# Moving the first weight columns to float32 loads with casts on chip, turning a batch's tails on TensorE, holding back small loads, and issuing the output weights a step earlier, in a fused attention and feed-forward kernel

## The chip, the cores and the metric

The kernel runs on one core of one Trainium2 chip. The metric is the device time of one execution in microseconds (us). Several executions of each kernel were taken, and each experiment ran beside the kernel before on the same chip. Times inside an execution are counted from the start of its span in the profile. Engines: PE is TensorE, DVE is VectorE, ACT is ScalarE, POOL is GpSimd, SP is SyncE (which only issues transfers here); PEld stands for TensorE's weight loads. L412 is line 412 of that kernel's source; the same line has other numbers in other kernels. PSUM is the memory into which PE writes its results.

## The reference, cut to what matters

Eight batches of causal attention over 8 heads of 64, with 576 queries and 16 extra "beacon" keys and values in front of 576 keys, then a gated feed-forward layer on all 4608 rows:

```python
scores = q @ concat(beacon_k, k).T / sqrt(64)      # causal mask on the 576 x 576 part
x = softmax(scores) @ concat(beacon_v, v)          # all heads side by side: 4608 x 512
out = (relu(x @ w_gate) * (x @ w_val)) @ w_out     # 512 -> 1536 -> 512
```

All inputs are float32 in HBM. The kernel computes with bfloat16 (bf16) operands, so that every input has to be cast once.

## The kernel before

PE is to be busy all the time. Batch one's attention runs alone in seven "steps"; then some up-projections of the first 512 rows run alone (`ALONE`) while batch two's inputs arrive; from then on attention steps of the next batch and pieces of the feed-forward layer take turns on PE. `after(s, f)` puts work at the end of step `s`, `mid[s]`, `between[s]` and `behind[s]` put it inside a step. Each engine runs its own instructions in the order in which they are written.

The parts that the change and the argument touch (cuts marked `...`):

```python
def load_w(dst, src, n0, n1, groups=(0, 1)):        # casting load: float32 -> bf16 on its way,
    for g in groups:                                # issued by GpSimd
        nc.gpsimd.dma_start(dst[:, 2*g:2*g+2, n0:n1], src[2*g*P:2*(g+1)*P, n0:n1]...)

ALONE = ((0, 3, 3, 3), (4, 4))     # up-projections in the steps between batch one and batch two
...
first.beacon = first.load_rows(beacon_k[0])         # SyncE's queue, float32
for i in range(2): ...  first.load_quarter(n, i, g) # keys and queries, rows 0 to 511
for t in range(NKT): first.load("v", t)
...
def load_first_tails():                             # rows 496 to 575 of keys and queries
    tails["k"] = first.load_cast_rows(k[0, :, 496:])   # casting loads by GpSimd
    tails["q"] = first.load_cast_rows(q[0, :, 496:])
def turn_first_tails():
    for n, dst in (("k", first.kT4), ("q", first.qT4)):
        nc.sync.dma_start_transpose(dst[:, :, :rows], h[:rows])
    second.beacon = second.load_rows(beacon_k[1])   # batch two's small loads
    load_tails(second)
after(0, turn_first_tails)
...
after(1, lambda: load_w(wg, moe_w_gate, 0, 384))
mid[3] = lambda: load_w(wv, moe_w_val, 0, 384)
after(3, lambda: first.cast("v", 4, pool))
mid[5] = lambda: load_w(wg, moe_w_gate, 384, 768, (0,))
mid[6] = lambda: load_w(wg, moe_w_gate, 384, 768, (1,))
after(6, lambda: load_w(wv, moe_w_val, 384, 768))
for n0 in (768, 1152): ...                          # after(6): the other columns, both weights
after(6, lambda: load_second(0))                    # batch two's keys and queries: 4 casting loads
after(7, lambda: load_second(1))                    # 4 more
for t in range(NKT):
    after(7, lambda t=t: second.load("v", t, t == 0))         # held: see below
for t in range(NKT):
    after(s2 - 1 + t // 2, lambda t=t: second.cast("v", t, pool))
after(s2 - 1, lambda: load_wo(0, 6))                # output weights, two casting loads of 768 KB
after(s2, lambda: load_wo(6, 12))                   # s2: batch two's first step
```

A "held" load has a one-element `memset` by GpSimd on its target first, so that SyncE cannot issue it before GpSimd has got there.

## Time and profile before

| | before |
|---|---|
| median of the first 3 runs | 395.1 us (394.35 to 395.18) |
| span of the profiled run | 392.3 us |
| PE busy | 369.8 us |
| PE idle | 22.5 us (span less busy), 10.8 of it in gaps of over 0.3 us in the first 110 us |
| time at half clock in the first 110 us | 6.8 us |

A part of the 22.5 us may not be idle time: the trace has 4235 matmuls for 4291 weight loads, so the records of 56 matmuls are missing. From the gaps after 110 us (3.7 us here) I estimate about 3 us.

From the page of the kernel before: busy time by engine; then PE's busy tenths and the granted clock of TensorE in 40 slices of 9.8 us; then the chain that ended last, by engine.

```profile
PE 369.8 (94%) x4235; PEld 188.2 (48%) x4291; DVE 206.2 (53%) x340; ACT 190.6 (49%) x266; POOL 130.0 (33%) x224
...
PE   7949996999999999999999999999999999999994
...
PEclk9999998999999999999999999999999999999998
...
PE 84%; DMA 8%; issue 3%; POOL 2%; SPq 1%; DVE 1%; ACT 0%; POOLq 0%; DVEq 0%
```

The digits 4 and 6 in PE's row are the third and the seventh slice, near 20 to 30 and 60 to 70 us. The view of waits, for PE in the first 110 us, names them (engine, line, what was waited for: us in total, times, longest):

```profile
PE f L477 <- DMA wo<-in_moe_w_out_dram: 3.5, 1, 3.5
PE os L412 <- issue: 3.5, 1, 3.5
PE s L362 <- DMA qT<-half: 1.7, 1, 1.7
```

The second of them is odd. PE's timeline (start, duration, engine, line, operation, tiles, count, idle time before it) shows it inside the matmuls of one chunk, whose operands were all there:

```profile
24.56 0.25 PE L412 MATMUL ab<-e,v 128*32 128x80 bf16 x8
28.29 0.26 PE L412 MATMUL os<-e,ones 128*32 128x80 bf16 x4 [3.48 <-issue]
```

The last mask (`AFFINE_SELECT`) ends at 25.7 us, and from 26.4 us on GpSimd issues one casting load after the other:

```profile
25.26 0.46 POOL L378 TENSOR_SCALAR_AFFINE_SELECT e<-e 128x320 bf16<-128x320 bf16 x1 [0.60 <-ACT e L370]
...
26.40 1.42 POOL L337 DMA_DIRECT2D wv<-in_moe_w_val_dram  x2
27.82 1.43 POOL L337 DMA_DIRECT2D wg<-in_moe_w_gate_dram  x2
```

The chain of waits in order of time between 40 and 70 us (start, us, what):

```profile
42.48 0.09 POOL raw L241
...
42.97 5.62 DMA raw<-in_v_dram
...
49.11 1.23 POOL v L259 x2
...
54.21 10.57 DMA wo<-in_moe_w_out_dram
...
64.82 2.29 PE f L477 x6
```

GpSimd's `memset` lets the values of batch two go, GpSimd casts them, and only then issues the second half of the output weights, for which PE waits.

The windows view has, for each stretch, the busy time of each engine (with counts), the granted clock, the DMA share and GB/s. With the stops at 24.8 and 61.3 us the clock is halved (0.50) for 3.4 us, from 27.7 and from 65.3 us:

```profile
28.00:31.00 3.00, 2.50 (x90) 1.90 (x92) 1.94 (x4) 0.00 (x0) 3.00 (x5) 0.50 1.17 151
65.00:68.50 3.50, 3.50 (x26) 1.32 (x28) 0.00 (x0) 1.34 (x2) 2.57 (x5) 0.54 0.91 204
```

### The profile page before, as it was taken

The numbers are of one execution on the slowest core, as the hardware profiler recorded it, in microseconds if no ns is written. First come the engines' busy times: TensorE is split into PE (matmuls) and PEld (weight loads), VectorE is DVE, ScalarE is ACT, GpSimd is POOL, SyncE is SP. The second block draws the span as 40 slices with busy tenths as digits, with TensorE's granted clock in tenths as the row PEclk, the third lists the DMA queues.
The fourth block names the chain that finished last, engine by engine and source line by source line (L and its number), as shares of the span: only waits on it lengthen the run. The fifth ranks groups of instructions, "written<-read, shape, count | busy, mean of one in ns | idle before, by whom it ended". The sixth has DMA issues, their size and how long they took to land.

```text
span 392.3 us, 10180 instructions
## 1 busy us (share of the span) xinstructions
PE 369.8 (94%) x4235; PEld 188.2 (48%) x4291; DVE 206.2 (53%) x340; ACT 190.6 (49%) x266; POOL 130.0 (33%) x224
## 2 busy tenths in 40 slices
PE   7949996999999999999999999999999999999994
PEld 3534452544555454544554445454545454444443
DVE  4746661663665665465646664655465555512420
ACT  4742373434755654555555554565465543323321
POOL 1987284251752335233514351426020200000000
PEclk9999998999999999999999999999999999999998
DMA  8999999978995994489438933994300020011002
GB/s 215 177 143 179 197 209 209 196 176 167 184 159 152 209 166 127 123 177 178 101 117 173 210 90 104 191 190 99 104 28 2 2 82 27 2 54 56 0 28 85
DMA packets 148835, 49.91 MB, mean 127 GB/s; under 512 B 134320, under 2 KB 144304, under 8 KB 148784
## 3 DMA queue, kind: packets, MB, share of 16 engines
q1 hardware_dynamic: 137328, 43.27, 52.4%
q0 software_dynamic: 11456, 5.93, 11.7%
q8 instruction: 35, 0.57, 0.6%
q14 instruction: 16, 0.13, 0.1%
HBM read 38.34 MB, written 9.44 MB: 122 GB/s over the span
## 4 chain that ended last, share of the span: by engine, by line
PE 84%; DMA 8%; issue 3%; POOL 2%; SPq 1%; DVE 1%; ACT 0%; POOLq 0%; DVEq 0%
PE f L477 24%; PE f L458 22%; PE s L467 12%; PE f L467 11%; PE ab L412 6%; PE s L362 6%; DMA wo<-in_moe_w_out_dram 3%; PE os L412 3%; DMA raw<-in_v_dram 1%; DMA wide<-in_q_dram 1%; DMA qT<-half 1%; DMA half<-in_k_dram 1%; POOL v L259 1%; POOL e L378 1%; SPq L622 0%
## 5 line engine op out<-in xcount | busy, mean ns | idle before, releaser
L370 ACT ACTIVATE e<-s 128x1024 bf16<-128x1024 f32 (+2 forms) x112 | 104.8, 964 | 18.7 <-PE s L362 18.4
L461 ACT ACTIVATE g<-f 128x512 f32<-128x512 f32 x108 | 64.6, 598 | 93.4 <-PE f L458 90.5
L458 PE MATMUL f<-xT,wg 128*128 128x512 bf16 x399 | 107.3, 380 | 2.6 <-issue 1.1
L378 POOL TENSOR_SCALAR_AFFINE_SELECT e<-e 128x512 bf16<-128x512 bf16 (+2 forms) x80 | 47.0, 598 | 168.5 <-ACT e L370 163.6
L477 PE MATMUL f<-wo,hT 128*128 128x512 bf16 (+1 forms) x425 | 96.0, 375 | 5.6 <-DMA wo<-in_moe_w_out_dram 3.5
L424 DVE RECIPROCAL r<-os 128x80 f32<-128x80 f32 (+2 forms) x43 | 57.6, 1340 | 60.2 <-PE os L412 60.1
L469 DVE TENSOR_TENSOR hT<-g,s 128x512 bf16<-128x512 f32 x56 | 38.5, 687 | 55.6 <-PE s L467 54.6
L467 PEld LDWEIGHTS <-wv 128*128 128x128 bf16 x432 | 42.3, 98 | 51.5 <-issue 1.2
L477 PEld LDWEIGHTS <-hT 128*128 128x128 bf16 x444 | 42.0, 98 | 51.5 <-issue 4.3
L458 PEld LDWEIGHTS <-wg 128*128 128x128 bf16 x432 | 39.6, 98 | 46.4 <-issue 1.1
L480 ACT COPY ob<-f 128x512 f32<-128x512 f32 (+1 forms) x37 | 21.3, 575 | 76.3 <-PE f L477 76.3
L469 DVE TENSOR_TENSOR hT<-g,f 128x512 bf16<-128x512 f32 x52 | 35.8, 688 | 42.3 <-PE f L467 37.8
L467 PE MATMUL s<-xT,wv 128*128 128x512 bf16 x222 | 57.2, 379 | 0.1
L467 PE MATMUL f<-xT,wv 128*128 128x512 bf16 x207 | 53.2, 379 | 0.3
L412 PE MATMUL ab<-e,v 128*32 128x80 bf16 (+4 forms) x1320 | 39.6, 234 | 0.2 <-POOL e L378 0.2
L263 POOL CAST half<-raw 128x512 bf16<-128x512 f32 (+2 forms) x60 | 36.6, 633 | 6.3 <-DMA raw<-in_q_dram 2.2
L362 PE MATMUL s<-qT,kT 64*128 64x80 bf16 (+3 forms) x704 | 35.7, 235 | 2.5 <-DMA qT<-half 1.7
L412 PE MATMUL os<-e,ones 128*32 128x240 bf16 (+4 forms) x660 | 32.4, 233 | 3.5 <-issue 3.5
L362 PEld LDWEIGHTS <-kT 64*128 64x128 bf16 x704 | 20.5, 97 | 26.8 <-issue 23.4
L412 PEld LDWEIGHTS <-v 128*32 128x32 bf16 (+1 forms) x1408 | 27.0, 100 | 9.4 <-issue 5.2
L259 POOL CAST v<-raw 128x512 bf16<-128x512 f32 (+1 forms) x40 | 26.7, 672 | 13.1 <-DMA raw<-in_v_dram 13.0
L437 DVE TENSOR_TENSOR xT<-ab,r 128x480 bf16<-128x480 f32 (+2 forms) x45 | 24.9, 554 | 0.8
(63 smaller groups left out, 138.9 us busy)
## 6 DMA issues: line engine op xcount, KB each, us to landing
out_dram<-ob SPq DMA_DIRECT2D x35, 256.0 KB, 2.2
raw<-in_q_dram SPq DMA_DIRECT2D x25, 256.0 KB, 4.8
raw<-in_v_dram SPq DMA_DIRECT2D x24, 256.0 KB, 4.8
raw<-in_k_dram SPq DMA_DIRECT2D x19, 256.0 KB, 4.6
raw<-in_v_dram SPq DMA_DIRECT2D x8, 224.0 KB, 4.3
wg<-in_moe_w_gate_dram POOLq DMA_DIRECT2D x8, 192.0 KB, 6.2
wv<-in_moe_w_val_dram POOLq DMA_DIRECT2D x8, 192.0 KB, 6.5
wo<-in_moe_w_out_dram POOLq DMA_DIRECT2D x2, 768.0 KB, 10.0
```

Source lines behind the costliest of these rows:

```text
L259: copy(self.v[:n, t].rearrange("p (h a d) -> p h a d", a=2, d=C), raw[:n].rearrange("p (h d a) -> p h a d", a=2, d=C))
L263: copy(h[:n], raw[:n])
L362: nc.tensor.matmul(self.s[:, a, c + j * n:c + (j + 1) * n], kT[rows, 2 * g + j, k0:k0 + P], qT[rows, 2 * g + j, q0:q0 + n], start=True, st ...
L370: nc.scalar.activation(e[:, :k * 4 * n].rearrange("p (k a x) -> p a k x", k=k, a=2), self.s[:, :, :k * 2 * n].rearrange("p a (k x) -> p a ...
L378: nc.gpsimd.affine_select(out=cols[:, :, :m], in_=cols[:, :, :m], pattern=[[0, 4], [1, m]], compare_op=ALU.is_ge, fill=0.0, base=base, cha ...
L412: nc.tensor.matmul(o[:, q0 - cq0:q0 - cq0 + n], w, e[:kr, 2 * (hh % 2) + hh // 2], start=(i == 0 and part != 1), stop=(i == self.last), sk ...
L424: nc.vector.reciprocal(self.r[:, :n], self.os[:, :n])
L458: nc.tensor.matmul(g[:, :n], wg[:, ki, nf * P:(nf + 1) * P], x[:, ki], start=(ki == 0), stop=(ki == KM - 1))
L461: nc.scalar.activation(gs[:, :n], g[:, :n], AF.Relu)
L467: nc.tensor.matmul(u[:, :n], wv[:, ki, nf * P:(nf + 1) * P], x[:, ki], start=(ki == 0), stop=(ki == KM - 1))
L469: nc.vector.tensor_mul(self.h[:, nf, c0:c1], gs[:, :n], u[:, :n])
L477: nc.tensor.matmul(o[:, n], self.h[:, nf, ms * P:(ms + 1) * P], wo[:, nf, n], start=(nf == 0), stop=(nf == NF - 1))
```

## The change

Its intent: the first weights should not wait for GpSimd, which has masks and casts to do; so 256 columns of both come early on SyncE's queue as float32 and are cast on chip. The tails of batch one are turned by PE, not by the DMA transpose. Batch two's small loads should not stand in the way of the early loads. One up-projection less stands before batch two, and the output weights are issued one step earlier. The core of the diff:

```diff
-        def load_rows(self, srcs):
+        def load_rows(self, srcs, held=False):
+            if held:
+                nc.gpsimd.memset(raw[:1, :1], 0.0)
...
+    def load_w_raw(src, n):      # two float32 loads by SyncE, 256 KB each
+    def cast_w(dst, raws, n, g, cast): ...
...
-    ALONE = ((0, 3, 3, 3), (4, 4))
+    ALONE = ((0, 3, 3, 2), (4, 4))
...
-        for t in range(NKT):
+        for t in range(2):
             first.load("v", t)
+        first.tails = [first.load_rows(k[0, :, 496:]), first.load_rows(q[0, :, 496:])]
+        for t in range(2, NKT):
+            first.load("v", t)
+        raw_g = load_w_raw(moe_w_gate, 256)
+        raw_v = load_w_raw(moe_w_val, 256)
...
-            load_first_tails()
...
-        after(0, turn_first_tails)       # DMA transposes, and batch two's small loads
...
         def cast_last():
             for n in "kq":
                 first.cast_quarter(n, 1, 1, dve)
+            cast_tails(first, dve)
+        def turn_first_tails(): ...      # PE transposes into one PSUM tile
         behind[1] = cast_last
         between[2] = lambda: [turn_first(n, 1, 1, dve)() for n in "kq"]
+        behind[2] = turn_first_tails
+        after(2, lambda: [held.pop(0)() for _ in range(2)])       # moves by ACT
-        after(1, lambda: load_w(wg, moe_w_gate, 0, 384))
...
-        mid[3] = lambda: load_w(wv, moe_w_val, 0, 384)
-        after(3, lambda: first.cast("v", 4, pool))
-        mid[5] = lambda: load_w(wg, moe_w_gate, 384, 768, (0,))
-        mid[6] = lambda: load_w(wg, moe_w_gate, 384, 768, (1,))
-        after(6, lambda: load_w(wv, moe_w_val, 384, 768))
+        mid[3] = lambda: load_w(wg, moe_w_gate, 256, 768, (0,))
+        after(3, lambda: load_w(wg, moe_w_gate, 256, 768, (1,)))
+        after(4, lambda: first.cast("v", 4, dve))
+        after(4, lambda: cast_w(wg, raw_g, 256, 0, dve))
+        after(4, lambda: cast_w(wg, raw_g, 256, 1, pool))
+        after(5, lambda: cast_w(wv, raw_v, 256, 0, pool))
+        after(6, lambda: cast_w(wv, raw_v, 256, 1, pool))
+        after(6, lambda: load_w(wv, moe_w_val, 256, 768))
+        def load_small():
+            second.beacon = second.load_rows(beacon_k[1], True)    # held
+            load_tails(second)
+        after(6, load_small)
...
-        after(s2 - 1, lambda: load_wo(0, 6))
-        after(s2, lambda: load_wo(6, 12))
+        after(s2 - 2, lambda: load_wo(0, 6))
+        after(s2 - 1, lambda: load_wo(6, 12))
```

More of the change, by code (lines that the diff above doesn't have):

```diff
@@ L310, in load_rows @@
             return raw, n
-        def load_cast_rows(self, srcs):
-            n = srcs.shape[1]
-            h = half.tile([P, d_model], BF16, name="half")
-            nc.gpsimd.dma_start(h[:n].rearrange("p (h d) -> p h d", d=D),
-                                srcs.rearrange("h p d -> p h d"))
-            return h, n
         def cast_rows(self, loaded, cast):
@@ L339, in load_w, with cast_w @@
                 src[2 * g * P:2 * (g + 1) * P, n0:n1].rearrange("(p a) n -> p a n", a=2))
+    def load_w_raw(src, n):
+        raws = []
+        for g in range(2):
+            raws.append(stage.tile([P, d_model], FP32, name="raw"))
+            nc.sync.dma_start(raws[g].rearrange("p (a n) -> p a n", a=2),
+                              src[2 * g * P:2 * (g + 1) * P, :n].rearrange(
+                                  "(p a) n -> p a n", a=2))
+        return raws
+    def cast_w(dst, raws, n, g, cast):
+        cast(dst[:, 2 * g:2 * g + 2, :n], raws[g].rearrange("p (a n) -> p a n", a=2))
     def load_wo(i0, i1):
@@ L603, in turn_next @@
             first.cast_quarter("q", 1, 0, dve)
-        tails = {}
-        def load_first_tails():
-            tails["k"] = first.load_cast_rows(k[0, :, 496:])
-            tails["q"] = first.load_cast_rows(q[0, :, 496:])
         def turn_third():
-            load_first_tails()
             held.pop()()
@@ L618 @@
         behind[0] = lambda: turn_first("q", 1, 0, dve)()
-        def turn_first_tails():
-            for n, dst in (("k", first.kT4), ("q", first.qT4)):
-                h, rows = tails[n]
-                nc.sync.dma_start_transpose(dst[:, :, :rows], h[:rows])
-            second.beacon = second.load_rows(beacon_k[1])
-            load_tails(second)
-        after(0, turn_first_tails)
         after(0, lambda: first.cast("v", 0, pool))
@@ L632, in cast_last, with turn_first_tails @@
                 first.cast_quarter(n, 1, 1, dve)
+            cast_tails(first, dve)
+        def turn_first_tails():
+            ps = f_ps.tile([P, 2, NP, 80], BF16, name="f")
+            for x, (h, dst) in enumerate(zip(first.tails, (first.kT4, first.qT4))):
+                held.append(first.turn_rows(h, dst[:, :, :80], act, ps[:, x]))
         behind[1] = cast_last
         between[2] = lambda: [turn_first(n, 1, 1, dve)() for n in "kq"]
-        after(1, lambda: load_w(wg, moe_w_gate, 0, 384))
+        behind[2] = turn_first_tails
+        after(2, lambda: [held.pop(0)() for _ in range(2)])
         after(2, lambda: first.cast("v", 2, pool))
         after(2, lambda: first.cast("v", 3, pool))
-        mid[3] = lambda: load_w(wv, moe_w_val, 0, 384)
-        after(3, lambda: first.cast("v", 4, pool))
-        mid[5] = lambda: load_w(wg, moe_w_gate, 384, 768, (0,))
-        mid[6] = lambda: load_w(wg, moe_w_gate, 384, 768, (1,))
-        after(6, lambda: load_w(wv, moe_w_val, 384, 768))
+        mid[3] = lambda: load_w(wg, moe_w_gate, 256, 768, (0,))
[10 more added lines that the diff above has]
+        after(6, load_small)
         for n0 in (768, 1152):
```

## The prediction

> **What bounds the kernel.** By the page, TensorE (PE) is busy 369.8 of 392.3 us and PE work is 84% of the chain that ended last, so only PE's idle time (22.5 us) and its time at a reduced clock can be won. The PE timeline and the waits put most of it into the first 70 us:
> 1. PE waits 1.67 us, from 20.3, for the DMA transpose of the query tail (chain: 1.56 us of issuing, 5.24 us of DMA).
> 2. PE stops for 3.48 us at 24.8 amid one chunk's matmuls, put down to "issue", with all operands there. The packets of the instruction queue show a 16 KB fetch that starts only at 25.8 and lands at 26.7, between weight packets of the software queue (GpSimd's DMAs). The Trainium skill ("Runtime: NRT & Kernel Launch", Instruction fetch mechanics) says that instructions are refilled in 16 KiB blocks of 256; PE had run about 480 since the fetch before. I read this stop as a late fetch.
> 3. PE waits 3.51 us at 61.3 for the second half of the output weights, issued at 54.2 and 10.6 us on their way.
> After stops 2 and 3 the granted clock is about 0.50 in 28 to 31 us and 0.57 in 65 to 69 us (windows): an estimated 1.2 and 1.7 us lost. Together 11.6 us: the ceiling.
>
> **What the change does.** The tails come as float32 rows, are cast by VectorE (about 0.4 us each), turned by PE (16 short matmuls) and moved by ScalarE (two copies, 0.45 us each, estimated from 0.59 us for 512 columns): both transposes and two casting DMAs (0.86 and 0.73 us of issuing on GpSimd) go. The first 256 columns of both weights are 1 MB on SyncE's queue, after the values, in place of four casting DMAs (0.71 us of issuing each); GpSimd gets three casts of about 0.64 us and gives one to VectorE. Batch two's small loads leave the early queue. One up-projection moves out of the stretch before batch two; the output weights are issued one step earlier and needed one step later.
>
> **On the critical path.**
> - Stop 1 goes (-1.7), but ScalarE is nearly full there (7.9 of 10 us in 10 to 20) and gets 0.9 us of copies: I count -0.7.
> - Stop 2: fewer software packets are under way, but the next columns are still issued about then. Even chances of a fetch on time: -2.5 with its clock loss.
> - Stop 3 goes with its slow clock: -5.2.
> - New waits: GpSimd's queue carries about 3.1 MB (bf16) from the value weights' column 256 to batch two's first keys and queries; at the 185 to 200 KB/us that it reached in 34 to 38 us that ends about 41 us, while PE, starting the feed-forward at 27.5 to 29, wants them about then: +1. The output weights now share the DMA engines with batch two's values: +0.8.
> The later part (80 to 390 us, PE over 97% busy) should not change.
>
> **Predicted: 388.5 us** (-6.6), range 384.5 to 393.5. Chances: faster by over 2% 0.36, within 2% 0.60, slower 0.04.
>
> **What would show it.** No DMA transpose in the first 25 us; no PE wait for output weights near 60 us; granted clock near 1.0 in 60 to 70; feed-forward's first matmul at 27.5 to 29 (31.1 before); PE's busy time down 1 to 3 us (clock), its idle time about 5.
>
> **What would make it wrong.** A late fetch again, with PE stopped 3 us; PE waits for the value weights' columns from 256 or batch two's keys; GpSimd's casts delay the masks; or the waits are given back when batch two starts, because the DMA engines, over 80% busy until 60 us, are the real limit: then 392 or more.

## The result, and the profile after

| | before | after |
|---|---|---|
| median of 4 runs | 395.14 us | 397.33 us (396.49 to 398.07) |
| span of the profiled run | 392.3 us | 396.4 us |
| PE idle in gaps over 0.3 us, first 110 us | 10.8 us | 12.4 us |
| half clock in the first 110 us | 6.8 us | 10.2 us |
| first feed-forward matmul | 31.1 us | 29.7 us |
| first down-projection matmul | 59.8 us | 71.5 us (one up-projection more stands before it) |

The ratio is 1.006, with a 95% interval of 1.0035 to 1.0084. Ratios here are the mean time of one kernel's fast runs over that of the other's of the same rounds, so they are not quite the ratios of the medians quoted. The kernel became 0.6% slower where 1.7% faster had been predicted. The profiled run of the changed kernel is the slowest of its four.

The same lines of the page after the change:

```profile
PE 374.1 (94%) x4243; PEld 189.8 (48%) x4299; DVE 204.9 (52%) x344; ACT 192.2 (48%) x268; POOL 127.7 (32%) x221
...
PE   7889669999999999999999999999999999999995
...
PEclk9999698999999999999999999999999999999999
...
PE 72%; DMA 13%; issue 5%; SPq 4%; POOL 3%; ACT 1%; DVE 1%; POOLq 0%; ACTq 0%
```

All three stops of before are gone. Two new weak slices stand at 40 to 60 us, the clock row has a 6 at 40 to 50 us, and 13% of the last chain is DMA where it was 8%. The view of waits for PE in the first 110 us:

```profile
PE ab L420 <- POOL e L386: 3.4, 2, 3.1
PE f L325 <- ACT g L469: 2.8, 1, 2.8
...
PE f L325 <- DVE kT L301: 1.3, 1, 1.3
```

**The wait of 3.1 us at 56.6 us** is for masks by GpSimd. **The wait of 2.8 us at 40.3 us** is put down to ACT, and that is misleading: it is a PE transpose of batch two's small loads (L325), and these had to be cast first. The waits of DVE between 10 and 50 us and of POOL between 10 and 70 us show what both engines really waited for:

```profile
DVE half L317 <- DMA raw<-in_q_dram: 3.1, 2, 2.8
```

```profile
POOL v L259 <- DMA raw<-in_v_dram: 12.5, 4, 9.6
```

The chain in order of time joins them (27 to 62 us of the changed kernel; start, us, what):

```profile
27.85 0.48 POOL e L386
28.32 0.56 POOL wv L347
28.88 1.37 POOL wv L332 x2
30.25 0.10 POOL raw L309
...
31.48 9.89 DMA raw<-in_q_dram
...
41.40 0.03 DVE half L317
...
46.65 0.09 POOL raw L241
...
47.13 9.83 DMA raw<-in_v_dram
...
57.10 0.88 POOL v L259 x2
...
59.08 0.60 POOL e L386
```

Read it from the top. GpSimd's last mask ends at 28.3 us (25.7 before), then comes a new cast, and only then the casting loads of the value weights' columns 256 to 768. Next it lets the small loads go (L309). The query tail is 9.89 us under way among the casting loads, DVE stands still for it, with a cast and then the reading of PE's results (`hT`) behind it in its order, and PE stops. GpSimd has issued all casting loads at 46.6 us and lets the values go (L241), but has issued the first half of the output weights at once (at 46.68 us in its timeline). The first large load of values (112 rows, 224 KB) takes 9.83 us (5.62 before).

The windows view shows what it cost: no transfer at all for 2 us, and two stretches at half clock (`0.50` before the DMA share).

```profile
28.00:30.00 2.00, 1.58 (x64) 1.09 (x65) 1.93 (x5) 0.31 (x1) 2.00 (x4) 1.00 0.00 0
...
43.30:50.00 6.70, 5.78 (x52) 3.24 (x51) 3.10 (x11) 0.60 (x1) 3.46 (x6) 0.50 1.75 182
...
60.30:63.60 3.30, 2.86 (x20) 1.10 (x21) 2.31 (x2) 1.20 (x2) 3.30 (x7) 0.50 1.04 156
```

The third wait, 1.3 us at 15.9 us, is where stop 1 went. DVE's timeline in the changed kernel: after the casts of the last keys and queries it waits for both tails to land, and only then copies the turned keys and queries out of PSUM (L301); PE waits for that copy before it turns the tails.

```profile
12.79 1.61 DVE L285 CAST hwide<-raw 128x512 bf16<-128x512 f32 x2
15.09 0.67 DVE L317 CAST half<-raw 80x512 bf16<-80x512 f32 x1 [0.70 <-DMA raw<-in_k_dram]
16.02 0.46 DVE L317 CAST half<-raw 80x512 bf16<-80x512 f32 x1 [0.26 <-DMA raw<-in_q_dram]
16.40 0.67 DVE L301 COPY kT<-f 128x512 bf16<-128x512 bf16 x1
```

That gave four theories, each with a rival:

- **P (priority):** the earlier output weights take the DMA engines from batch two's values. Rival R: the DMA engines are the limit anyway and the order only moves the wait.
- **H (held):** the held small loads come too late. Rival: holding them is harmless.
- **Q (queue start):** the string of casting loads that GpSimd begins after its last mask decides when batch two's data are there. Rival S: its start doesn't matter.
- **T (tails):** stop 1 was given back as DVE's and PE's wait for the tails. Rival: ACT sets the start of the feed-forward.

And for stop 2, the late instruction fetch: the software queue's weight packets (my prediction), or the DMA transposes, or both together.

### The profile page after: what moved, and what is told of

Same layout as the page of the kernel before. It is cut to its first block, busy times and chain, and to the rows that moved or that the text cites. A ratio compares the mean times of both kernels' runs of the same rounds, so it can differ in the third digit from the quotient of the medians.

```text
span 396.4 us, 10219 instructions
## 1 busy us (share of the span) xinstructions
PE 374.1 (94%) x4243; PEld 189.8 (48%) x4299; DVE 204.9 (52%) x344; ACT 192.2 (48%) x268; POOL 127.7 (32%) x221
## 4 chain that ended last, share of the span: by engine, by line
PE 72%; DMA 13%; issue 5%; SPq 4%; POOL 3%; ACT 1%; DVE 1%; POOLq 0%; ACTq 0%
PE f L485 19%; PE f L466 19%; PE s L475 11%; PE f L475 8%; PE s L370 6%; PE ab L420 6%; DMA raw<-in_q_dram 4%; DMA raw<-in_v_dram 4%; DMA raw<-in_k_dram 3%; PE os L420 2%; DMA kT<-half 2%; SPq L244 2%; SPq L281 1%; ACT e L378 1%; SPq L310 1%
## 5 line engine op out<-in xcount | busy, mean ns | idle before, releaser
L466 PE MATMUL f<-xT,wg 128*128 128x512 bf16 x405 | 110.3, 383 | 2.3 <-DMA hwide<-in_k_dram 0.7
L485 PE MATMUL f<-wo,hT 128*128 128x512 bf16 (+1 forms) x424 | 94.8, 373 | 1.6 <-issue 0.8
L386 POOL TENSOR_SCALAR_AFFINE_SELECT e<-e 128x512 bf16<-128x512 bf16 (+2 forms) x80 | 47.3, 603 | 150.7 <-ACT e L378 142.4
L432 DVE RECIPROCAL r<-os 128x80 f32<-128x80 f32 (+2 forms) x43 | 57.6, 1339 | 56.5 <-PE os L420 56.5
L477 DVE TENSOR_TENSOR hT<-g,s 128x512 bf16<-128x512 f32 x60 | 41.3, 688 | 69.0 <-PE s L475 67.9
L485 PEld LDWEIGHTS <-hT 128*128 128x128 bf16 x444 | 41.9, 98 | 47.3
L466 PEld LDWEIGHTS <-wg 128*128 128x128 bf16 x432 | 39.7, 98 | 47.6 <-issue 2.1
L475 PE MATMUL s<-xT,wv 128*128 128x512 bf16 x238 | 62.3, 383 | 0.2
L477 DVE TENSOR_TENSOR hT<-g,f 128x512 bf16<-128x512 f32 x48 | 33.0, 688 | 35.3 <-PE f L475 30.6
L475 PE MATMUL f<-xT,wv 128*128 128x512 bf16 x186 | 49.0, 381 | 0.7 <-ACT qT L301 0.2
L420 PEld LDWEIGHTS <-v 128*32 128x32 bf16 (+1 forms) x1408 | 26.7, 98 | 13.3 <-issue 7.9
L370 PEld LDWEIGHTS <-kT 64*128 64x128 bf16 x704 | 20.5, 97 | 25.8 <-issue 23.6
L259 POOL CAST v<-raw 128x512 bf16<-128x512 f32 (+1 forms) x39 | 25.6, 662 | 15.1 <-DMA raw<-in_v_dram 14.4
```

Of the source, the lines that this page charges most:

```text
L259: copy(self.v[:n, t].rearrange("p (h a d) -> p h a d", a=2, d=C), raw[:n].rearrange("p (h d a) -> p h a d", a=2, d=C))
L370: nc.tensor.matmul(self.s[:, a, c + j * n:c + (j + 1) * n], kT[rows, 2 * g + j, k0:k0 + P], qT[rows, 2 * g + j, q0:q0 + n], start=True, st ...
L386: nc.gpsimd.affine_select(out=cols[:, :, :m], in_=cols[:, :, :m], pattern=[[0, 4], [1, m]], compare_op=ALU.is_ge, fill=0.0, base=base, cha ...
L420: nc.tensor.matmul(o[:, q0 - cq0:q0 - cq0 + n], w, e[:kr, 2 * (hh % 2) + hh // 2], start=(i == 0 and part != 1), stop=(i == self.last), sk ...
L432: nc.vector.reciprocal(self.r[:, :n], self.os[:, :n])
L466: nc.tensor.matmul(g[:, :n], wg[:, ki, nf * P:(nf + 1) * P], x[:, ki], start=(ki == 0), stop=(ki == KM - 1))
```

## The experiments

### Mends one at a time in the changed kernel, and one part alone

**a1_wo_late**: the output weights as before.

```diff
-        after(s2 - 2, lambda: load_wo(0, 6))
-        after(s2 - 1, lambda: load_wo(6, 12))
+        after(s2 - 1, lambda: load_wo(0, 6))
+        after(s2, lambda: load_wo(6, 12))
```

> The changed kernel, with the two output-weight loads issued one step later, as before the change. Theory P (the early output-weight load takes the DMA engines from batch two's values): the values, issued at 47 us and landed at 57 in the changed kernel, land by about 52; PE's wait of 3.1 us for the masks at 56.6 goes to under 1 us and so does the slow clock in 60 to 64 us; no new wait for the output weights over 1 us; about 393 us. Rival R (the DMA engines are the limit, the order of loads only moves the wait): PE waits about as long for the output weights near 66 us instead; 396.5 to 398 us.

396.05 us (ratio 1.0027 to the kernel before, 0.9994 to 1.006). The first two large loads of values landed at 52.8 and 53.9 us (57.0 and 57.6 in the changed kernel), the wait for the masks and the second stretch of half clock were gone, and no wait of over 0.5 us for the output weights came. P's mechanism is right. The gain was smaller than either the waits or I had said: the wait for the small loads grew to 3.7 us in this run, and a PE wait of 1.5 us for masks appeared at 100 us. The total is nearer to what R had written (396.5 to 398) than to P's 393; it is the waits that speak for P.

**a2_small_free**: the small loads not held.

```diff
-            second.beacon = second.load_rows(beacon_k[1], True)
+            second.beacon = second.load_rows(beacon_k[1])
```

> The changed kernel, with batch two's small loads no longer held (one memset less), so that SyncE issues them at about 19.5 us, behind the weights. Theory P (held back, they fall among ten casting weight loads and the query tail takes 9.9 us, for which VectorE stops): the tail lands by 26 us, VectorE's wait of 2.8 us at 38.6 and PE's of 2.8 us at 40.3 go, and so does most of the slow clock in 43 to 50 us; but PE then waits about 2 us for batch two's keys and the values' wait stays: 395 to 396.5 us. Rival R (holding them back is harmless): within 0.5 us of the changed kernel, 397 us.

396.68 us (ratio 1.0042, 1.001 to 1.0074). The wait at 40 us went, as H says. But PE then waited 1.9 us in four pieces between 43.2 and 46.3 us for batch two's keys and queries, and 3.2 us for the masks as before, with half clock after both. One hurdle taken away, PE ran into the next. The total lies 0.65 us under the changed kernel's median, close to what both theories had written, so only the waits speak for H here.

**a3_both**: both edits.

> Both edits of the two runs before this one. Theory P: the gains add up, 390.5 to 392.5 us, under the kernel before. Rival R: 396 us or more, as the DMA engines set the time at which batch two's data are there.

394.99 us (ratio 0.9998, 0.9969 to 1.0028): level with the kernel before, better than either alone, and short of what I expected. PE's largest waits in the first 110 us:

```profile
PE f L325 <- DVE kT L301: 3.5, 1, 3.5
PE s L300 <- DMA hwide<-in_k_dram: 2.5, 2, 2.1
```

The first is the wait for the tails (T), 3.5 us in this run, with 6.8 us of half clock behind it; the second the wait for batch two's keys (Q).

**b1_tails_pe**: the kernel before with one part of the change alone, the tails by SyncE's float32 loads, DVE casts and PE; no DMA transposes, everything else as before.

```diff
+        first.tails = [first.load_rows(k[0, :, 496:]), first.load_rows(q[0, :, 496:])]
...
-                nc.sync.dma_start_transpose(dst[:, :, :rows], h[:rows])
+            cast_tails(first, dve)                 # behind[1]
+        behind[2] = turn_first_tails               # PE
+        after(2, lambda: [held.pop(0)() for _ in range(2)])
```

> The kernel before, with one part of the change alone: the tails loaded as float32 rows and turned by PE, no DMA transposes; weights, output weights, plan and unheld small loads as before. If the software queue's weight packets made the instruction fetch late (stop 2), PE still stops about 3.5 us near 25 us and only the 1.7 us wait goes: 394 to 395 us. If the DMA transposes made it late, the stop goes, the feed-forward starts at 28 us or earlier (31.1 before) and the slow clock in 28 to 31 us is gone: 391 to 392.5 us if nothing gives it back.

397.66 us (ratio 1.0074, 1.0042 to 1.0106), slower than both of my cases. Both early stops are gone, and the first feed-forward matmul comes at 29.9 us, 1.2 us earlier than before. Yet:

```profile
PE f L485 <- DMA wo<-in_moe_w_out_dram: 3.5, 1, 3.5
PE f L325 <- DVE kT L301: 2.2, 1, 2.2
PE s L300 <- DMA hwide<-in_k_dram: 1.5, 2, 1.2
```

The wait for the tails (2.2 us) delays batch one's exponentials, these the masks, and these GpSimd's loads: the value weights up to column 768 are issued by 29.9 us (27.1 before), batch two's first half of keys and queries lands at 46.6 us (44.1), and the output weights at 68.0 us (64.8). So PE was earlier and had to wait longer. In the kernel before, PE began to turn batch two's keys at 44.3 us and the last of them landed at 44.1: PE had been just in time. From these times I infer that a gain of PE alone in the first 30 us turns into a wait at 44 us; b1 does not isolate this, as its loads also came later. The run e1 below is the cleaner test.

### Queue start and tails in the changed kernel, and the other part alone

**a4_wv_early**: the value weights' columns 256 to 768 after step 4.

```diff
-        after(6, lambda: load_w(wv, moe_w_val, 256, 768))
...
+        after(4, lambda: load_w(wv, moe_w_val, 256, 768))
         after(5, lambda: cast_w(wv, raw_v, 256, 0, pool))
```

> The changed kernel, with the two casting loads of the value weights' columns 256 to 768 issued after step 4 instead of after step 6, behind the last masks. In the changed kernel GpSimd issues them at 28.8 us, the DMA engines move nothing between 28 and 30 us, and the queue of 10 weight loads and 8 key and query loads that follows ends at 51.6 us, against 47.4 before the change. Theory Q (that queue is a chain whose start sets when batch two's data are there): they are issued by 26 us, the hole is filled, batch two's keys and queries all land by about 49 us and the values by about 54.5; PE's waits at 40 and 57 us shrink by about 2 us each; 393 to 395 us. Rival S (the queue's start doesn't matter, the two waits come from the held small loads and the early output weights alone): batch two's loads land within 1 us of the changed kernel's and the time stays within 1 us of 397.

396.64 us (ratio 1.0042, 1.0012 to 1.0072). They were issued by 24.3 us, batch two's first half landed at 44.3 us (48.4 in the changed kernel) and all of it at 47.6 us (51.6): Q, and not S. The wait at 40 us shrank to 0.3 us. But PE was earlier at the masks now, and waited 4.6 us there, with 6.8 us of half clock; the values had landed only at 52.9 us, behind the early output weights. So the loads did what Q says, while the total stayed where S had put it (within 1 us of 397).

**a5_tails_later**: DVE copies the last keys and queries before it casts the tails, and PE turns the tails one step later.

```diff
                 first.cast_quarter(n, 1, 1, dve)
-            cast_tails(first, dve)
...
-        between[2] = lambda: [turn_first(n, 1, 1, dve)() for n in "kq"]
-        behind[2] = turn_first_tails
-        after(2, lambda: [held.pop(0)() for _ in range(2)])
+        def turn_last():
+            for n in "kq":
+                turn_first(n, 1, 1, dve)()
+            cast_tails(first, dve)
+        between[2] = turn_last
+        behind[3] = turn_first_tails
+        after(3, lambda: [held.pop(0)() for _ in range(2)])
```

> The changed kernel, with the casts of the first batch's tails put behind the copies of the last keys and queries on VectorE, and their turning by PE one step later. In the changed kernel and the runs so far VectorE waits for the tails to land before those copies, and PE waits 1.3 to 3.5 us at 13 to 17 us behind it. Theory T (stop 1 was given back as this wait): the wait goes to under 0.4 us, the first feed-forward matmul moves from 29.7 to 28 us or earlier; the total follows by 1 to 2 us if nothing later gives it back: 395 to 396.5. Rival: ScalarE, nearly full, sets the start of the feed-forward, and it stays at 29 us or later.

396.52 us (ratio 1.0045, 1.0013 to 1.0076). The feed-forward started at 27.8 us (29.7), so ACT did not set it. A PE wait of 1.2 us was left, for another tile of the same PSUM pool, so T's "under 0.4 us" was wrong. The total followed little (1.0045 against the changed kernel's 1.006): PE waited 1.7 us for the small loads and 4.4 us for the masks.

**b2_weights_f32**: the kernel before with the other part alone, the float32 weights with their casts and the changed order of the later columns.

> The kernel before, with one part of the change alone: the first 256 columns of both weights as float32 on SyncE's queue with casts on chip, the later columns in the changed kernel's order; DMA transposes and casting loads of the tails, plan, output weights and unheld small loads as before. On stop 2: if the DMA transposes (or the tails' casting loads) made the instruction fetch late, PE stops again for 2 to 4 us between 22 and 30 us, with no weight packets on the software queue before 21 us; if the software queue's weight packets did, PE does not stop. Theory Q: the queue of casting loads starts late (about 29 us) and batch two's keys and queries land at 49 us or later, 2 us or more after the kernel before; 397 to 400 us in all.

397.63 us (ratio 1.007, 1.003 to 1.0109). The value weights up to column 768 were issued by 30.4 us and batch two's first half of keys and queries landed at 47.3 us, 3.2 us after the kernel before (all of it at 50.8, against 47.4). The core of the change, put into the kernel before, makes it slower by 0.7%. How much of that is the later start of the casting loads is not separated: the DMA transposes now stood behind the float32 weights on SyncE's queue, and PE waited 4.4 us for them, and 3.8 us for the output weights. Of stop 2 see below.

**c1_all**: all four mends in the changed kernel.

> The changed kernel with all four mends: output weights one step later, small loads not held, value weights' columns 256 to 768 issued after step 4, tails' casts and turning later. Theories P, Q and T together: no PE wait of over 1.5 us in the first 100 us, slow clock in at most one stretch, first feed-forward matmul at 28 us or earlier, 388.5 to 391.5 us, clearly under both kernels. If the DMA engines are the limit in any order: 393.5 us or more.

391.76 us (391.0 to 393.37), ratio 0.9915, 0.9884 to 0.9945: clearly under both kernels, and just above the range that I had written down. PE's largest waits in the first 110 us (left out: the 1.5 us before the first matmul), and the window in which nothing was transferred in the changed kernel:

```profile
PE ab L420 <- POOL e L386: 2.8, 4, 1.0
...
PE f L325 <- DVE r L437: 1.3, 1, 1.3
...
PE f L485 <- DMA wo<-in_moe_w_out_dram: 1.0, 1, 1.0
```

```profile
28.00:30.00 2.00, 2.00 (x9) 0.86 (x9) 0.64 (x2) 0.60 (x1) 2.00 (x4) 1.00 1.17 172
```

No wait reaches 1.5 us, there is no half clock before 388 us, and the first half of batch two's keys and queries landed at 43.7 us. The feed-forward started at 28.2 us, not by 28. PE still stood idle for 9.7 us in gaps of over 0.3 us in the first 110 us (10.8 before, 12.4 in the changed kernel): they are many and short now, and none of this stretch is at half clock (6.8 and 10.2 us).

### Each mend taken back, and stop 2

| run | taken back in c1 | median us | ratio to before (95%) | PE in the first 110 us |
|---|---|---|---|---|
| c1_all | nothing | 391.76 | 0.9915 (0.9884 to 0.9945) | no wait of 1.5 us, no half clock |
| l1_wo_back | output weights | 393.63 | 0.9965 (0.9927 to 1.0002) | 4.6 us for masks, 6.8 us half clock (but see below) |
| l2_small_back | small loads | 392.31 | 0.9948 (0.9912 to 0.9985) | 0.8 and 0.9 us near 39 us, 2.2 us for output weights, twice 3.4 us half clock |
| l3_wv_back | value weights | 393.19 | 0.9948 (0.9914 to 0.9983) | 1.9 us in four pieces for keys, 2.1 us in turning the tails, 1.8 us for output weights, twice 3.4 us half clock |
| l4_tails_back | tails | 393.32 | 0.9948 (0.9911 to 0.9985) | 2.9 us for tails, 1.6 us for output weights, 1.7 us for masks, no half clock |
| c2_quota3 | the plan | 393.81 | 0.9954 (0.9915 to 0.9994) | 4.1 us for output weights, 6.8 us half clock |
| e1_tails_later_cast_w | float32 weights, early value weights and plan (see below) | 395.95 | 1.0026 (0.9981 to 1.007) | 3.4 us for output weights, 1.7 us for keys, twice 3.4 us half clock |

The intervals of the single steps overlap that of c1, so each step by itself is shown by its waits, not by its total. A closer comparison is d1 (below), which is c1 with two transposes for nobody and ran on the chip of l1, l2 and l3: 390.49 to 392.0 us, ratio 0.9892 (0.9853 to 0.993). The means of the three lie 1.7 to 2.2 us above its mean.

A long wait in one profile is not a price, either. The profiled execution of l1 took 391.51 us, one of its two fast ones (the other four took 393.07 to 395.06). It has the 4.6 us wait and the half clock, and yet it was faster than c1's profiled execution (392.18 us): its idle time in gaps of over 0.3 us in the first 110 us was 9.6 us against c1's 9.7. And d1 had a wait of 2.7 us for the output weights. The waits show what is linked to what; what one mend is worth in the total is not shown.

**l1_wo_back** puts the output weights one step earlier again.

> The kernel with all four mends (c1), with the output weights issued one step earlier again, as the change has it. Theory P: batch two's values land 3 us or more later than in c1 (where the first three parts land by 47.0, 47.8 and 48.7 us), PE waits 3 us or more for the masks behind them, and a stretch of half clock of 3.4 us or more follows: 394 to 396 us, 2.5 us or more over c1. Rival R: within 1 us of c1.

The first two large loads of values landed at 50.5 and 51.4 us (47.8 and 48.7 in c1), and PE's largest wait is:

```profile
PE ab L420 <- POOL e L386: 4.6, 1, 4.6
```

P's wait and half clock came as expected; the values' delay (2.75 us) and the total (1.9 us over c1's median, on another chip) were a little under what I had written.

**l2_small_back** holds the small loads again.

> The kernel with all four mends (c1), with batch two's small loads held back again, as the change has it. As the queue of casting loads now starts earlier, the query tail should land by 37 us as in the run with the value weights early alone, close to where VectorE wants it: PE waits at most 1 us, and the time is within 1.2 us of c1 (391 to 393 us). If holding them back is harmful by itself, PE waits 2 us or more near 39 us: 394 us or more.

0.55 us over c1's median; the query tail landed at 36.9 us. PE waited 0.8 and 0.9 us near 39 us, more than the 1 us that I had allowed, and less than the 2 us of the other case. By these waits the held loads hurt where the casting loads start late, and less where they start early.

**l3_wv_back** issues the value weights after step 6 again.

> The kernel with all four mends (c1), with the value weights' columns 256 to 768 issued after step 6 again, as the change has it. Theory Q: the queue of casting loads starts 2 us or more later than in c1 with nothing moved for 2 us before it; the first half of batch two's keys and queries lands at 45 us or later (43.7 in c1), PE waits about 2 us in all for them and gets a stretch of half clock: 393.5 to 395.5 us. Rival S: within 1 us of c1.

Batch two's first half landed at 46.5 us (43.7), and PE waited for it and got its half clock: Q again. The total is 0.3 us under the range that I had written.

**l4_tails_back** casts and turns the tails as the change does.

> The kernel with three mends, the tails cast and turned as the change has it. Theory T: VectorE waits for the tails before it copies the last keys and queries, PE waits 1.5 us or more at 13 to 17 us, the feed-forward starts at 29 us or later (28.2 in c1), and everything behind it moves by about 1 us: 392.5 to 394 us. Rival: within 0.5 us of c1.

PE waited 2.9 us and the feed-forward started at 30.2 us, as T says.

**c2_quota3** restores `ALONE = ((0, 3, 3, 3), (4, 4))`.

> The kernel with all four mends, with the plan as before (3, 3, 3 up-projections before batch two instead of 3, 3, 2). Batch two then needs its data 1.7 us later and the first down-projection comes one step earlier, so PE waits 2 us or more for the output weights (1.0 us in c1): 392 to 393.5 us. If the plan does not matter: within 0.5 us of c1.

PE waited 4.1 us for the output weights, more than I expected, and the total is 0.3 us over my range. The changed plan is a good part of the change: it asks for the output weights later (first down-projection at 58.9 us here, at 61.3 us in c1).

**e1_tails_later_cast_w** is b1 with the tails as in a5: all weights by casting loads, plan and output weights as before, small loads not held.

> The kernel before with the tails turned by PE (as in b1), their casts and turning put later (as in a5), and all weights by casting loads as before: what is left of c1 without its float32 weights, its early value weights and its plan. If the float32 weights are what gives c1 its gain, 394 to 396 us, as the queue of casting loads is as long as before and PE waits 3 us again for the output weights; if the later tails give it, 391 to 393.

395.95 us: 1.0026 of before, 0.9981 to 1.007. PE waited 3.4 us for the output weights. Against c1 it lacks the float32 weights, the early value weights and the plan. So these three together are worth something (about 1.1% by the two ratios) once the rest is in order; how much of it is the float32 weights alone was not tried. Against the kernel before, e1 is also the test of my sum: stops 1 and 2 are gone and the feed-forward starts at 27.9 us, 3.2 us earlier, but the value weights up to column 768 are issued no earlier (28.0 us, 27.1 before), the first half of batch two's keys and queries lands at 44.9 us (44.1), PE waits 1.7 us in all for the keys, and the total is no better.

### Stop 2, and the fastest version

**d1_transposes** and **d2_transposes_early** are c1 with two DMA transposes into a tile that nothing reads, behind the tails' casts (d1) or ahead of the float32 weights (d2).

```diff
+        spare = const.tile([P, 2, NP, 80], BF16, name="spare")
...
+            for x, (h, rows) in enumerate(first.tails):              # d1
+                nc.sync.dma_start_transpose(spare[:, x], h[:rows])
...
+        for x in range(2):                                           # d2
+            nc.sync.dma_start_transpose(spare[:, x], wo[:80, 0])
```

> The kernel with all four mends (c1), with two DMA transposes of the tails into a spare tile that nothing reads, issued by SyncE once VectorE has cast the tails, at about 17 to 19 us. On stop 2: so far PE's second instruction fetch starts within 1.5 us of PE's 450th instruction in the eight kernels without DMA transposes, and 6 us after it in the two with them. If the transposes themselves hold the fetch back, it starts 3 us or more after the 450th instruction here as well (at 24 us or later), and PE stops for 1 us or more near its 705th instruction without waiting for anything else; about 393 to 394.5 us. If not, the fetch comes within 1.5 us of the 450th instruction and PE doesn't stop.

> The kernel with all four mends (c1), with two DMA transposes (of a tile of ones into a spare tile that nothing reads) that SyncE issues at about 15 us, before the float32 weights, so that they move at about 17 to 22 us as in the kernel before; in the run with dummy transposes before this one they were still behind the weights when the fetch was made. On stop 2: if transposes under way hold the instruction fetch back, it starts 3 us or more after PE's 450th instruction (at 24 us or later). If it starts within 2 us of it, the transposes are not the cause, and the cause of stop 2 stays open between the other things that only the kernel before and the run with float32 weights alone have.

d1: 390.85 us, ratio 0.9892 (0.9853 to 0.993), no slower than c1. d2: one run of 393.28 us (state unknown). Neither had a stop of PE at a fetch.

**d3_packets** is c1 with more casting loads of weights issued early, so that their packets fill the stretch in which the fetch is asked for; **d4_packets_transposes** adds two transposes for nobody behind the first two float32 loads.

```diff
         for n0 in (768, 1152):
-            after(6, lambda n0=n0: load_w(wg, moe_w_gate, n0, n0 + 384))
-            after(6, lambda n0=n0: load_w(wv, moe_w_val, n0, n0 + 384))
+            after(1 if n0 == 768 else 6, lambda n0=n0: load_w(wg, moe_w_gate, n0, n0 + 384))
+            after(2 if n0 == 768 else 6, lambda n0=n0: load_w(wv, moe_w_val, n0, n0 + 384))
```

> The kernel with all four mends (c1), with the casting loads of columns 768 to 1152 of both weights issued after steps 1 and 2 (at about 17 and 20 us) instead of after step 6, so that the software queue's packets move from about 18 us on without a lull, and no DMA transposes. On stop 2: if such packets hold the instruction fetch back (my prediction's reading), the second fetch starts 3 us or more after PE's 450th instruction and PE stops near its 705th. If it starts within 2 us of it, packets alone are not the cause. The time is not what this run is for; about 391 to 394 us.

> The run with early weight packets, with two DMA transposes for nobody added after the first float32 weight loads, which take part in the same stretch. If it needs both, transposes and packets under way together, the second fetch is late here (3 us or more after PE's 450th instruction) and in time in the run with packets alone. If both are in time, neither kind of traffic brings the late fetch back and its cause stays open.

d4 was run once: 391.30 us (state unknown).

From the trace's packets of the instruction queue and the starts of PE's instructions: when PE ran its 450th instruction, when its second instruction fetch of the execution began (us), and how many of PE's instructions had started by then.

```
                        450th    second             started
                     instruction fetch   late by    by then  other transfers at that time
before                  19.71    25.80     6.1        705    transposes to 21.9; casting weight loads, with a lull at 25
b2 (float32 weights)    19.25    25.60     6.3        549    transposes to 24.1; casting weight loads from 20 to 25
b1 (tails by PE)        23.10    22.49    -0.6        428    none just then
changed kernel          22.92    22.87     0.0        444    end of the float32 weights
c1                      20.91    22.43     1.5        505    float32 weights, small loads
d1                      21.03    21.81     0.8        502    as c1; transposes land at 25.4 and 26.2
d2                      20.28    21.39     1.1        505    float32 weights; transposes land at 20.0
d3 (packets)            21.54    23.52     2.0        505    float32 and casting weight loads since 18
d4 (both)               22.58    25.42     2.8        532    the same since 19; transposes land at 24.5 and 24.7
```

The time since the 450th instruction, on which I had built my expectations, misleads for b2: PE stood idle there from 19.8 to 24.2 us, waiting for the transposes, so it had not come far. By count, b2's fetch began at 549 instructions, and in all 19 kernels other than the one before it began at 420 to 549. Only in the kernel before had PE started 705, the last of them just before its stop. So one profile of one kernel shows a late fetch; whether its other executions have it too is not shown. Neither transposes (d1, d2), nor casting loads (d3), nor the two together (d4) brought it back. PE's stop began at 24.8 us, the fetch at 25.8 us; it landed at 26.7 us and PE went on at 28.3 us. A late fetch fits this, but no run tested that it is what stopped PE, and the last 1.6 us are not explained. What made the fetch late stays open.

d3 has a second result, which I had not looked for: 389.38 us (388.87 to 389.77), ratio 0.9874 (0.9839 to 0.9909). It is the fastest version, 1.3% under the kernel before, with its interval wholly clear of one; it overlaps the intervals of c1 and d1, so that it is faster than these is not shown. From its page, and from its windows view:

```profile
PE 373.8 (97%) x4299; PEld 188.2 (49%) x4299; DVE 206.4 (53%) x344; ACT 191.8 (50%) x268; POOL 128.3 (33%) x220
```

```profile
21.00:25.00 4.00, 3.28 (x72) 2.36 (x68) 2.46 (x6) 2.23 (x4) 3.99 (x7) 0.50 1.21 258
```

(PE's 97% cannot be set against the 94% of the kernel before: no matmul record is missing here, x4299 for as many weight loads, and 56 are missing there.)

PE was slower early than in the other versions with the tails put later, except d4: it ran at half clock from 18.2 to 28.4 us, and the feed-forward started at 30.2 us, 2 us after c1's and even after the changed kernel's. But the DMA engines moved 258 GB/s from 21 to 25 us, batch two's first half of keys and queries landed at 40.7 us (43.7 in c1), the first two large loads of values at 45.7 and 46.6 us (47.8 and 48.7), and PE had no wait of over 0.7 us from 29 to 110 us. This agrees with Q: the casting loads were under way earlier, and fewer of them were left to issue after the last mask, which would make up for PE's slower pace before them.

## Why the prediction was wrong, point by point

- **"Only PE's idle time (22.5 us) and its time at a reduced clock can be won" and "together 11.6 us: the ceiling".** The sum was right, but I took the stops one by one as if each could be cut out of the total. They lie on different chains. Stops 1 and 2 were before batch two's data came in, and PE was just in time for those: 44.3 us, with the last landing at 44.1. e1 removed both stops and started the feed-forward 3.2 us earlier, and its time was that of the kernel before (ratio 1.0026, 0.9981 to 1.007); b1, whose loads also came later, was 0.7% slower. This is the step that failed first.
- **"GpSimd's queue ... ends about 41 us ... : +1".** The right term was on my list, and its size was wrong: it ended at 48.4 us in the changed kernel. Both its start and its rate were off. At 185 to 200 KB/us an end at 41 us means a start near 25 us (estimate). The loads begin when GpSimd is through with its last mask and the new cast, at 28.8 us (26.4 before), with nothing moved from 28 to 30 us; from 28.8 to 48.4 us the DMA engines moved 166 KB/us, the held small loads included. a4 and l3 show it: with the value weights issued 4 to 5 us earlier the data come 3 to 4 us earlier. In c1 the time from the first of these loads to the landing of batch two's first half is nearly the same as in the changed kernel (24.4 to 43.7, 19.3 us; 28.8 to 48.4, 19.6 us): what differs is the start.
- **"Stop 3 goes with its slow clock: -5.2".** It went, and a wait of 3.1 us for masks with 3.4 us of half clock took its place. I put the output weights' competition with the values at +0.8; with the loss at half clock (half of 3.4 us) it was about 4.8 (estimate). a1 and l1 show that the earlier issue causes the wait.
- **"Batch two's small loads leave the early queue."** I counted this as free. In the changed kernel the held query tail took 9.9 us, DVE stopped for it, PE waited 2.8 us and then ran 6.8 us at half clock. a2 removes the wait; in l2, where the casting loads start early, it is 0.8 and 0.9 us.
- **"Stop 1 goes (-1.7) ... I count -0.7".** It was given back as a wait for the tails on DVE (PE: 1.3 us, and 2.2 to 3.5 us in b1 and a3), because the tails' casts stand before copies that PE needs. The feed-forward began at 29.7 us, not at 27.5 to 29. ACT, which I blamed beforehand, was not the limit: a5 started it at 27.8 us. (The turning took 8 matmuls, not the 16 that I had counted.)
- **"Stop 2: even chances".** It went. The reading as a late instruction fetch fits the trace and was not tested. My cause, the software queue's packets, was not confirmed: d3 sent such packets through the stretch, and the fetch began after 505 instructions as in c1, not after 705. The cause is open. That the stop was worth nothing by itself I infer from e1, which had neither stop 1 nor stop 2; no run removed stop 2 alone.
- **"The waits are given back when batch two starts, because the DMA engines ... are the real limit: then 392 or more."** This was named as what would make it wrong, and it is close to what happened. But bandwidth was not the limit of the changed kernel: the same loads in another order are c1 and d3, 0.85% and 1.26% under the kernel before.

## What to carry to other kernels

Before adding up PE's stops, find for each the chain that ends in it, and ask what PE will wait for next if it arrives earlier. Where an engine issues a long string of loads in its program order, ask when it gets to the first of them, and how many are left to issue when it does. Place each load by when it is needed: an early issue of something big and not urgent can delay what is small and urgent (here 9.8 us for 224 KB instead of 5.6).

## What the Trainium skill lacked or had wrong

- "Runtime: NRT & Kernel Launch", Instruction fetch mechanics, says that the fetch of 16 KiB blocks is mostly hidden. The trace agrees on the blocks (35 packets of 16,384 bytes for 8,564 PE instructions that it shows, about one for 245). It lacks that a fetch can begin late: in the kernel before one began when PE had started 705 instructions, where the 19 other kernels have 420 to 549, and PE stopped for 3.48 us around it. The cause stays open here.
- "TensorE: Matmul & The Clock Gate", The HAM clock gate, gives a window of about 3.4 us and half rate after an idle one. The trace agrees on half clock, in stretches of 3.41, 6.83, 10.24 (d3) or 13.65 us (d4). It asks to avoid gaps of over about 3.4 us, and says further down that frequent short idle times between groups of matmuls can do the same, without sizes. The runs give some: half clock followed 0.8 and 0.9 us within 3 us near 39 us (l2), and 1.9 us in four pieces (l3), but not a single 2.9 us (l4).
- "DMA: Bandwidth & Descriptors", Queues, rings and completion order, says that each DMA engine takes packets from its queues in turn. It lacks what this means for loads with packets of unlike size. While the output weights (packets of 1024 bytes) ran beside the values (256 bytes) in the changed kernel, from 51 to 54 us, the two queues moved about as many packets (111 to 151 and 148 to 163 in each us) but 28 to 39 KB against 150 to 164 KB. (In the two us before, the values' queue moved fewer packets, 115 and 41 against 436 and 185, so equal numbers are not the whole of it; and these are the trace's packets, which need not be the page's.) A load of 224 KB took 9.8 us where it took 5.6 before.
